# A recurrent attention block with an MLP: new order of the weight stream and of the V bounces at the start, residual sums in four pieces at the MLP

## Chip, cores, metric

One core of one Trainium2 chip. The metric is the time of one execution in device microseconds (us). A time is the median of several executions; every execution quoted here, of every kernel, was in the fast state. Times within a profile count from the start of its span.

## The reference, cut to what matters

```python
# S = 2048 rows of 512, 32 heads of 128, M = 8 memory rows, segments of 32 rows: 64 segments
for s in range(n_seg):
    h = concat([mem, x[:, s*32:(s+1)*32]])           # 40 rows
    q, k, v = h @ Wq, h @ Wk, h @ Wv                   # 512 -> 32 heads x 128
    p = softmax(where(mask, q @ k.T * scale, -1e9))
    o = (p @ v) @ Wo                                   # 4096 -> 512
    mem = o[:, :M]                                     # the next segment needs it
    outs.append(o[:, M:])
h  = x + concat(outs)                                  # raw x here; the x in the loop is layer-normed
h2 = h + gelu(layernorm(layernorm(h)) @ w1 + b1) @ w2 + b2     # MLP, 1792 wide
```

The 64 segments are a chain, since each needs the memory rows of the one before. The kernel takes x in 16 blocks of 128 rows (four segments each); q, k and v of a block's x rows are computed a block ahead ("block passes"), those of the memory rows within the segment.

## The kernel before

Three things matter. First, **the start**: SP (SyncE's queue) loads the weights as sixteen pieces of 1 MB, WK, WV, WQ and WO, in that order and as fast as it can issue. PE (TensorE) works through START.

```python
START = (("B", "K", 0, (4, 6)), "K0", "K1", ("B", "K", 1, (4, 6)), ("B", "V", 0, (6, 7)), "V",
         ("B", "V", 1, (6, 7)), ("B", "Q", 0, (5, 6)), "Q0", "Q1", "Z",
         "SC0", "SC1", ("B", "Q", 1, (5, 4)), "PV0", "PV1", "SA", "WO")
...
load_x(0, load)
load(...m0...); load(...b1n...)
load_w(WK, wk_d, "WK")          # four pieces of 1024 KB
load_x(1, load)
load_w(WV, wv_d, "WV")
load_w(WQ, wq_d, "WQ")
for g in range(4): load(... WO[:, g*8:(g+1)*8, :] ..., 1024, ...)
for tb in (2, 3, 4): load_x(tb, load)
```

Second, **the bounce of V**. PV needs the V rows of a block in another layout than the matmul leaves them in. They are evicted to VSB, sent to HBM (v_last, four DMAs of 64 KB, the first leg) and read back as VBD (four more, the second leg; the leg's part number sg serves only segment 4*block + sg):

```python
def v_B_spread(bk):
    for i in range(4):
        S.dma(... vd[bk, :, i] <- VSB[:, i] ..., 64, reads=[("VSB", r) for r in range(2)],
              eng="act" if bk < 2 else "sp")
    for sg in range(4):
        S.dma(... VBD[:, bk % 2, sg] <- vd[bk] part sg ..., 64, reads=[("vd", bk, i) for i in range(4)],
              eng="act" if bk < 2 else "sp")
```

Third, **the residual sums at the MLP**: h + b2 for a block of 512 rows is one GpSimd instruction of 128x2048 elements; the first stands ahead of the MLP in the program, the second at its step fc 3 (fc counts the MLP's 14 pieces of 128 columns), and both run in the MLP's first 11 us.

```python
def p2_res(k):
    S.op("pool", lambda e: e.tensor_tensor(hb[:, k % 2], hx_of(k), b2b, ALU.add), ...)
```

Every operation is registered with its reads, writes and an estimated duration, and the program's own list scheduler fixes each engine's order from them. A small change therefore may reorder several engines.

## Time and profile before

| | before |
|---|---|
| median (range), first set | 908.75 us (906.79 to 914.81), 3 runs |
| span of the profile | 909.0 us |
| PE busy | 827.0 us, 91% |
| end of segment 0 (transposition of its WO result starts) | 69.76 us |
| end of segment 1 | 82.83 us |
| end of segment 63 | 789.08 us |
| first W1 matmul, 17th W2 matmul | 793.35 us, 817.09 us |

The span is a start of 83 us, a chain of 62 segments (11.04 to 12.97 us each, 11.4 in the mean), and an MLP that is bound by PE. Only the ends have slack. The prediction shows the lines that say so. One more view is needed later: the issues of SP in the timeline of the start (start, length of the issues together, operation, count). The issuing itself takes long: WQ's four issues 11 us and WO's 19.

```profile
11.32 11.02 SPq L520 DMA_DIRECT2D WQ<-in_A_Wq_dram  x4
22.39 19.09 SPq L531 DMA_DIRECT2D WO<-in_A_Wo_dram  x4
```

### The profile page before, as it was taken

What the parts mean: (1) busy time and instruction counts of PE and PEld (TensorE: products, weight loads), DVE (VectorE), ACT (ScalarE), POOL (GpSimd) and SP (SyncE); (2) the same over time, 40 slices, a digit from 0 to 9 for tenths busy, and PEclk for the clock granted to TensorE, in tenths of its full rate; (3) what the DMA queues carried; (4) which work ended last, traced back from release to release, by engine and by line L of the source; (5) the groups of instructions that cost most, each with busy time, mean ns of one, the idle gap of its engine ahead of it and who ended that gap; (6) DMA issues with size and microseconds to landing.
All of it is one profiled execution on the core that took longest, in us unless ns stands there. A gap on an engine that the chain in (4) does not pass through costs nothing.

```text
span 909.0 us, 47688 instructions
## 1 busy us (share of the span) xinstructions
PE 827.0 (91%) x22285; PEld 436.4 (48%) x21261; DVE 659.3 (73%) x1801; ACT 522.2 (57%) x1520; POOL 222.6 (24%) x293
## 2 busy tenths in 40 slices
PE   1638899999999999999999999999999998889998
PEld 0214455555545555545555545555555554444443
DVE  2328788888888988897888898888797988661111
ACT  1224676656666767665757666767665666534442
POOL 3014222232222222222222222222222223141100
PEclk9858999999999999999999999999999999999999
DMA  8930001010101010101010101010101110610000
GB/s 334 388 112 3 4 4 27 10 33 15 27 16 28 16 27 16 27 16 27 16 27 15 27 15 27 10 28 9 27 10 27 33 27 9 209 39 24 24 24 23
DMA packets 35301, 40.42 MB, mean 44 GB/s; under 512 B 2452, under 2 KB 31004, under 8 KB 35100
## 3 DMA queue, kind: packets, MB, share of 16 engines
q1 hardware_dynamic: 32892, 36.33, 12.0%
q8 instruction: 170, 2.79, 1.3%
q10 hardware_dynamic: 2208, 1.05, 0.4%
q14 instruction: 31, 0.25, 0.1%
HBM read 28.98 MB, written 8.39 MB: 41 GB/s over the span
## 4 chain that ended last, share of the span: by engine, by line
PE 71%; ACT 15%; DVE 7%; DMA 3%; issue 2%; ACTq 1%; SPq 0%; POOL 0%; DVEq 0%
PE ps L583 27%; PE ps L826 15%; ACT VS L605 7%; PE ps L595 7%; PE ps L367 6%; PE quad L1076 6%; PE ps L1069 5%; ACT EC L727 4%; ACT OT L605 3%; DVE kqT L625 2%; DMA v_last<-VSB 2%; PE quad L798 2%; PE quad L745 2%; DMA xr<-in_A_x_dram 1%; DVE WV L933 1%
## 5 line engine op out<-in xcount | busy, mean ns | idle before, releaser
L640 POOL TENSOR_SCALAR QA<-kqT 128x384 bf16<-128x384 f32 x128 | 150.2, 1174 | 478.3 <-PE ps L583 324.4
L625 DVE STREAM_TRANSPOSE kqT<-ps 128x512 f32<-128x512 f32 x320 | 218.1, 710 | 28.6 <-PE ps L583 18.7
L826 PE MATMUL ps<-WO,OT 128*32 128x256 bf16 x4224 | 154.4, 277 | 14.3 <-ACT OT L605 5.1
L605 ACT CAST KALL<-kqT 128x512 bf16<-128x512 f32 x160 | 98.6, 618 | 82.2 <-DVE kqT L625 80.8
L583 PE MATMUL ps<-WK,hT 128*32 128x512 bf16 x2048 | 134.9, 384 | 3.6 <-DVE hT L832 3.3
L583 PE MATMUL ps<-WQ,hT 128*32 128x512 bf16 x2048 | 134.4, 383 | 0.0
L605 ACT CAST OT<-quad 128x128 bf16<-128x128 f32 (+1 forms) x176 | 80.2, 456 | 81.7 <-PE quad L749 46.6
L826 PEld LDWEIGHTS ps<-WO,OT 128*32 128x32 bf16 x4224 | 96.7, 96 | 45.9 <-ACT OT L605 33.5
L595 PE MATMUL ps<-WV,hT 128*32 128x512 bf16 x1024 | 100.7, 382 | 0.9
L367 PE MATMUL ps<-WV,hT 128*32 128x512 bf16 x1024 | 99.9, 379 | 0.0
L583 PEld LDWEIGHTS ps<-WQ,hT 128*32 128x32 bf16 x2048 | 54.6, 98 | 58.5 <-issue 2.5
L727 ACT ACTIVATE EC<-ps,nmc 128x64 f32<-128x64 f32 x256 | 78.1, 314 | 0.6 <-DVE nmc L723 0.6
L605 ACT CAST VS<-ps 128x512 bf16<-128x512 f32 x127 | 68.2, 589 | 11.7 <-PE ps L583 2.6
L1072 ACT ACTIVATE WQ<-ps,b1t 128x512 bf16<-128x512 f32 x56 | 38.5, 688 | 62.1 <-PE ps L1069 61.6
L583 PEld LDWEIGHTS ps<-WK,hT 128*32 128x32 bf16 x2048 | 49.3, 97 | 49.6 <-DVE hT L832 4.6
L699 ACT COPY ps<-maskCF 128x128 f32<-128x128 f32 x122 | 32.8, 269 | 62.2 <-DVE kqT L625 33.7
L1120 DVE TENSOR_TENSOR WV<-quad,WV 128x512 bf16<-128x512 f32 x16 | 11.1, 692 | 74.3 <-PE quad L1076 74.3
L715 PEld LDWEIGHTS ps<-KALL,ZC 128*32 128x32 bf16 x2048 | 34.7, 97 | 57.5 <-ACT ZC L606 48.0
L838 DVE STREAM_TRANSPOSE TT<-ps 128x256 f32<-128x256 f32 x66 | 29.3, 444 | 37.8 <-PE ps L826 37.8
L1076 PE MATMUL quad<-WK,WQ 128*128 128x512 bf16 x224 | 56.1, 388 | 0.5 <-DVE xr L872 0.5
L595 PEld LDWEIGHTS ps<-WV,hT 128*32 128x32 bf16 x1024 | 27.3, 96 | 60.3 <-DVE kqT L625 29.9
L727 ACT ACTIVATION_READ_ACCUMULATOR EC<-ps,nmc 128x1 f32 x256 | 52.4, 205 | 0.0
(107 smaller groups left out, 1218.3 us busy)
## 6 DMA issues: line engine op xcount, KB each, us to landing
WK<-in_A_Wk_dram SPq DMA_DIRECT2D x4, 1024.0 KB, 6.9
WV<-in_A_Wv_dram SPq DMA_DIRECT2D x4, 1024.0 KB, 19.0
WQ<-in_A_Wq_dram SPq DMA_DIRECT2D x4, 1024.0 KB, 19.0
WO<-in_A_Wo_dram SPq DMA_DIRECT2D x4, 1024.0 KB, 15.3
v_last<-VSB SPq DMA_DIRECT2D x56, 64.0 KB, 2.1
VBD<-v_last SPq DMA_DIRECT2D x56, 64.0 KB
WK<-in_B_w_dram SPq DMA_DIRECT2D x2, 1792.0 KB, 13.2
xr<-in_A_x_dram SPq DMA_DIRECT2D x16, 128.0 KB, 2.1
```

What stands on the lines that cost most here:

```text
L367: return e.add_instruction(mybir.InstMatmult(name="I-%d" % (4000000 + _kept[0]), engine=mybir.EngineType.PE, start_tensor_calc=start, stop ...
L583: ins = e.matmul(ps[bank][32 * j:32 * j + 32, :], lhs(cc), rhs(W, r, cc, j), start=(cc == 0), stop=(cc == DC - 1), tile_position=(0, 32 * j))
L595: ins = e.matmul(o, l, m, start=(cc == 0), stop=(cc == DC - 1), tile_position=(0, 32 * j))
L605: return {"act": (lambda e: e.copy(out, src), t_act(n, ps_)), "dve": (lambda e: e.tensor_copy(out, src), 0.16 + 1.042e-3 * n * fast)}
L625: S.op("dve", lambda e: e.transpose(kqT[:, i, :], ps[bank][:, :]), reads=[("ps", bank)], writes=[("kqT", i)], dur=t_dve(512) + 0.02)
L640: S.op("pool", lambda e: e.tensor_scalar(QA[:, h0:h0 + 16, 0:NA], src[:, :, 0:NA], scale, None, ALU.mult), reads=[("kqT", i)], writes=[("Q ...
L715: ins = e.matmul(ps[bank][32 * j:32 * j + 32, 64 * sl:64 * sl + 64], ZC[:, par, h, :], rhs, start=False, stop=(i == 3), tile_position=(0, ...
L727: ins = e.activation(EC[:, r, sl, :], ps[bank][:, 64 * sl:64 * sl + 64], ACTF.Exp, bias=nmc[:, r, sl:sl + 1], accum_out=smc[:, r, sl:sl + 1])
L826: ins = e.matmul(ps[bank][32 * j:32 * j + 32, 0:256], lhs(slot(h)), wo_cols(h, b), start=(k == 0), stop=(k == 15), tile_position=(0, 32 * ...
L1069: ins = e.matmul(ps[bank][:, 0:SBT], W1[:, cc, fc * P:(fc + 1) * P], hnT_of(k)[:, cc, :], start=(cc == 0), stop=(cc == DC - 1))
L1072: S.op("act", lambda e: e.activation(gT[:, fc, :], ps[bank][:, 0:SBT], ACTF.Gelu_apprx_tanh, bias=b1t[:, fc:fc + 1], scale=1.0), reads=[(" ...
L1076: S.op("pe", lambda e: e.matmul(quad[:, t, :], gT[:, fc, t * P:(t + 1) * P], W2[:, fc, :], start=(fc == 0), stop=(fc == FC - 1)), reads=[" ...
```

## The change

Intent: let V go first, so that its bounce is hidden behind the other weights; take the bounce off ACT, which stood in its queue for it; keep no more than three weight pieces under way, so that a bounce is not queued behind ten of them; and take the long GpSimd sums out of the place where DVE normalizes for the MLP. The core of the diff; "..." and comments stand for what is cut:

```diff
-START = (("B", "K", 0, (4, 6)), "K0", "K1", ("B", "K", 1, (4, 6)), ("B", "V", 0, (6, 7)), "V", ("B", "V", 1, (6, 7)), ("B", "Q", 0, (5, 6)), "Q0", "Q1", "Z",
-         "SC0", "SC1", ("B", "Q", 1, (5, 4)), "PV0", "PV1", "SA", "WO")
+START = (("B", "V", 0, (6, 7)), "V", ("B", "K", 0, (4, 6)), "K0", "K1", ("B", "K", 1, (4, 6)), ("B", "Q", 0, (5, 6)), "Q0", "Q1", "Z",
+         "SC0", "SC1", ("B", "Q", 1, (5, 4)), "PV0", "PV1", "SA", ("B", "V", 1, (6, 7)), "WO")
...
         def load(fn, kb, writes):
-            first[0] = S.dma(fn, kb, writes=writes, behind=first[0])
+            after = [big[-3]] if kb > 1000 and len(big) > 2 else []     # at most three pieces under way
+            o = S.dma(fn, kb, writes=writes, after=after)
+            chain.append(o)
+            if kb > 1000:
+                big.append(o)
...
+        load_w(WV, wv_d, "WV")
+        load_x(1, load)
         load_w(WK, wk_d, "WK")
-        load_x(1, load)
-        load_w(WV, wv_d, "WV")
         load_w(WQ, wq_d, "WQ")
...
         # both legs of the bounce: eng="act" if bk < 2 else "sp" is gone, all on SP; kept in spread["out"/"in", bk]
...
+                for what, n in ((("in", 0), 11), (("out", 0), 8)):
+                    i = chain.index(big[n - 1]) + 1          # out: behind the 8th piece (WK's last)
+                    chain[i:i] = spread[what]                # in: behind the 11th (WQ's third)
+                chain += spread["out", 1] + spread["in", 1]
+                for a_, b_ in zip(chain, chain[1:]):
+                    b_.prev = a_
...
         # a WO unit reads only its own two of the four WO pieces
...
         def p2_res(k):
-            S.op("pool", ... hb[:, k % 2] <- hx_of(k) + b2b, after=used["WV"] + S.users([("PTA", (NS - 1) % 2)]), dur=t_pool(2048))
+            for t in range(TBS):
+                S.op("pool", ... hb[:, k % 2, t, :] <- hx_of(k)[:, t, :] + b2bc, after=used["WV"] + S.users([("rs2", NTB - 1)]), dur=1.1)
...
-        p2_res(0)                       # was ahead of the MLP; now every block's sums stand at fc 8,
...                                     # the next block's norms at fc 8 (3 before), its transposes at fc 12 (9 before)
```

More of the change, by code (lines that the diff above doesn't have):

```diff
@@ L510, in load_x @@
             load(lambda e: e.dma_start(xr[:, tb % XR, :], x_d[:, tb, :]), 128, writes=[("xr", tb % XR)])
-        first = [None]
+        big = []
         def load(fn, kb, writes):
-            first[0] = S.dma(fn, kb, writes=writes, behind=first[0])
+            after = [big[-3]] if kb > 1000 and len(big) > 2 else []
[3 more added lines that the diff above has]
+                big.append(o)
+        chain, spread = [], {}
         def load_w(W, wd, key):
@@ L672, in v_B_spread @@
                 o = vd[bk, :, i]
-                S.dma(lambda e, i=i, o=o: e.dma_start(o, VSB[:, i].rearrange("p r e -> p (r e)")), 64, reads=[("VSB", r) for r in range(2)], writes=[("vd", bk, i)],
-                      eng="act" if bk < 2 else "sp")
+                w = S.dma(lambda e, i=i, o=o: e.dma_start(o, VSB[:, i].rearrange("p r e -> p (r e)")), 64, reads=[("VSB", r) for r in range(2)], writes=[("vd", bk, i)])
+                spread.setdefault(("out", bk), []).append(w)
             for sg in range(4):
                 v = vd[bk].rearrange("(j s) i t n -> s j (i t) n", s=4)[sg]
-                S.dma(lambda e, sg=sg, v=v: e.dma_start(VBD[:, bk % 2, sg].rearrange("p r e -> p (r e)"), v), 64, reads=[("vd", bk, i) for i in range(4)], writes=[("VBD", bk % 2, sg)],
-                      eng="act" if bk < 2 else "sp")
+                w = S.dma(lambda e, sg=sg, v=v: e.dma_start(VBD[:, bk % 2, sg].rearrange("p r e -> p (r e)"), v), 64, reads=[("vd", bk, i) for i in range(4)], writes=[("VBD", bk % 2, sg)])
+                spread.setdefault(("in", bk), []).append(w)
         def build_masks(bank_c, bank_a):
@@ L828, in f @@
                     return ins
-                S.op("pe", f, reads=[("WO", g) for g in range(4)] + reads(q // 4), writes=[("ps", bank)], dur=0.22, mode=MC, ni=16)
+                S.op("pe", f, reads=[("WO", 2 * (q // 4) + g) for g in range(2)] + reads(q // 4), writes=[("ps", bank)], dur=0.22, mode=MC, ni=16)
         def halves_add(tt, q2, out, cols):
@@ L908, in build_kernel @@
         hnT0 = bass.AP(kq45.tensor, kq45.offset, [list(kq45.ap[0]), [SBT, DC], [1, SBT]])
-        b2b = bass.AP(b2bc[:].tensor, b2bc[:].offset, [list(b2bc[:].ap[0]), [0, TBS], [1, D]])
         used = {"WQ": [], "WK": [], "WV": []}
@@ L936, in p2_res @@
         def p2_res(k):
-            S.op("pool", lambda e: e.tensor_tensor(hb[:, k % 2], hx_of(k), b2b, ALU.add), reads=[("hx", bf_of(k)), "b2bc"], writes=[("hb", k % 2)],
-                 after=used["WV"] + S.users([("PTA", (NS - 1) % 2)]), dur=t_pool(2048))
+            for t in range(TBS):
+                S.op("pool", lambda e, t=t: e.tensor_tensor(hb[:, k % 2, t, :], hx_of(k)[:, t, :], b2bc[:], ALU.add), reads=[("hx", bf_of(k)), "b2bc"],
+                     writes=[("hb", k % 2, t)], after=used["WV"] + S.users([("rs2", NTB - 1)]), dur=1.1)
         def p2_T(k, half, bank):
@@ L1108, in build_kernel @@
                         p2_load(k + 1)
-                    if fc == 3 and k + 1 < NSB:
+                    if fc == 8:
+                        p2_res(k)
+                    if fc == 8 and k + 1 < NSB:
                         p2_norm(k + 1)
-                        p2_res(k + 1)
-                    if fc == 9 and k + 1 < NSB:
+                    if fc == 12 and k + 1 < NSB:
                         p2_T(k + 1, 0, 7)
@@ L1120, in build_kernel @@
                 S.op("dve", lambda e, t=t, bf=bf: e.tensor_tensor(ob[:, bf, t, :], quad[:, t, :], hb[:, bf, t, :], ALU.add),
-                     reads=[("ps", t), ("hb", bf)], writes=[("ob", bf, t)], after=used["WV"], dur=t_dve(512))
+                     reads=[("ps", t), ("hb", bf, t)], writes=[("ob", bf, t)], after=used["WV"], dur=t_dve(512))
                 S.dma(lambda e, tb=tb, t=t, bf=bf: e.dma_start(out_d[:, tb, :], ob[:, bf, t, :]), 128, reads=[("ob", bf, t)], writes=[("out", tb)])
```

## The prediction

> **What bounds the kernel now.** First the page's part 2, 40 slices of 22.7 us, to find where TensorE is not the limit:
>
> ```profile
> PE   1638899999999999999999999999999998889998
> ...
> PEclk9858999999999999999999999999999999999999
> DMA  8930001010101010101010101010101110610000
> ```
>
> TensorE is 90% busy or more from slice 6 on. It is not in slices 1 to 5, where the DMA engines are full (8, 9) and then idle while PE is still at 3 and its clock at 5, and again in slices 34 to 36 (750 to 818 us), where the MLP begins. The change touches just these two places. In between lie 63 recurrent segments: the chain that ended last shows the same two V evictions in each, 11.05 to 11.2 us apart, and nothing in the diff shortens that.
>
> For the start I read busy time by stretches of 2 us (columns: stretch, length, busy time of PE, PEld, DVE, ACT, POOL, clock, DMA share, GB/s):
>
> ```profile
> 34.00:36.00 2.00, 1.04 (x16) 0.33 (x16) 0.72 (x1) 0.00 (x0) 0.00 (x0) 1.00 1.03 391
> ...
> 48.00:50.00 2.00, 0.00 (x0) 0.00 (x0) 0.00 (x0) 0.02 (x1) 0.00 (x0) 0.50 1.11 344
> ...
> 54.00:56.00 2.00, 0.00 (x0) 0.00 (x0) 0.00 (x0) 0.00 (x0) 0.00 (x0) 0.50 0.20 65
> ...
> 68.00:70.00 2.00, 1.72 (x35) 1.08 (x24) 1.52 (x6) 0.00 (x0) 0.79 (x2) 0.50 0.00 0
> ```
>
> Until 36 us weights come at about 400 GB/s; the stream ends at about 51 us. Yet no engine works between 48 and 58 us, and the clock stays halved to 75 us. So the stream sets the floor, and something else costs time beyond it. What that is stands in the chain of waits (start, length, what):
>
> ```profile
> 32.70 6.60 DMA v_last<-VSB
> ...
> 39.39 0.59 ACT VSB L605
> ...
> 46.72 9.08 DMA v_last<-VSB
> ...
> 58.22 0.64 ACT QTB L606
> ...
> 60.10 3.44 PE ps L583 x32
> ...
> 66.15 3.59 PE ps L826 x48
> ```
>
> The V rows of a block go to HBM and back (VSB to v_last to VBD). For blocks 0 and 1 ACT issues both legs. It stands in its own queue until the first leg has landed, and the evictions behind it wait too: VSB of block 1 to 39.39, and QTB of block 0, whose input was ready by 46, to 58.22. ZC, the scores and all of segment 0 hang on QTB. The waits view agrees: ACT QTB waited 14.4 us in two waits, the longest 10.2, named "issue".
>
> For the other end, the timeline of the MLP's beginning:
>
> ```profile
> 795.98 4.06 POOL L937 TENSOR_TENSOR WV<-xr,b2bc 128x2048 f32<-128x2048 bf16 x1 [10.90 <-DVE PTA L789]
> 796.73 8.19 DVE L933 TENSOR_SCALAR WV<-WQ,agg,rst 128x512 bf16<-128x512 bf16 x4
> ...
> 805.48 1.38 DVE L933 TENSOR_SCALAR WV<-WQ,agg,rst 128x512 bf16<-128x512 bf16 x4
> ...
> 810.16 0.40 PE L863 MATMUL quad<-ident,opT 128*128 128x128 bf16 x4 [2.87 <-DVE opT L854]
> ...
> 811.07 5.31 PE L1076 MATMUL quad<-WK,WQ 128*128 128x512 bf16 x16 [0.51 <-DVE xr L872]
> ```
>
> The same four normalizations take 8.19 us beside two residual sums on POOL (to 804.1) and 1.38 us without. The DVE work that PE needs (opT, TTB) is late by that much: PE stands still 2.87 and 0.51 us, and then runs 16 matmuls in 5.31 us at a clock that the stretches give as 0.52 and 0.63.
>
> **What the Trainium skill says.** (1) "DMA: Bandwidth & Descriptors", section "Anatomy of one DMA": DMA engines do not wait on semaphores; a wait happens on the issuing sequencer before dispatch. The trace agrees: the whole ACT queue stood 9.08 us. (2) Same page, "Queues, rings and completion order": each engine consumes a ring's descriptors in ring order. So behind SP's weights a bounce will not be quick either; a cap of 3 MB bounds the queue ahead of it. Here 64 KB legs took a median of 9.8 us to land in the start and 2.1 later. (3) "SBUF — State Buffer", section "SBUF: two separate sides": DVE in a two-port mode and GpSimd share a port pair by an exclusive lock, and the loser blocks for the whole instruction. The trace agrees: L933 lasts 407 ns in the median and 4160 at most, a POOL sum 4060. (4) "TensorE: Matmul & The Clock Gate", Part 1: half clock after an idle window of some 3.4 us, full clock after one of sustained work. Here 32 matmuls take 1.90 us in the start when warm and 3.44 at 60 us.
>
> **The change, part by part.**
>
> (a) V first, ACT freed, bounces in SP's queue. The bytes stay, so I count landings. The GB/s of the 2 us stretches, summed, give 4.0 MB by 14 us, 8.9 by 26, 13.0 by 36 and 17.2 by 48; a landing is seen about 2 us later (x1, the last of 4.46 MB, landed at 17.17, the sum reaches that at 15.1). In the new order: WV complete near 16.5 us (4.3 MB), WK near 27 (8.9 MB with x1 and the first leg), WQ near 39 (13.4 MB with both legs), WO near 51 (17.6 MB).
>
> V of block 0 ends about 0.9 us after WV (8 cold matmuls); with 0.6 for the eviction VSB stands by 18.2. The first leg's slot comes after WK's last piece is issued, which waits for WK's first to land (about 19.5); four issues of 0.6 us are done at 22 and land near 27.5. The second leg (four of 0.53) is issued near 30 and lands before WQ does, long before PV needs it. Neither slot leaves fewer than about two pieces (2 MB, 5 us) under way, so I expect no hole in the stream.
>
> PE from WQ on, in its order: Q of block 0, last 8 matmuls, at 39.0 to 39.9; Q0 and Q1, 32 matmuls, cold 3.5 us (warm 1.9), to 42.5; transpose 0.72 and ZC 0.30, scores to 44.7; softmax (0.28, 1.0, 0.17, 0.3, 0.3 and hops) to 47, beside Q of block 1; PV, SA to 49.5; V of block 1, 32 matmuls now warm 1.9, to 51.5; WO, 64 matmuls at 1.93 warm or 3.6 cold, from 51.5 since its last piece lands near 51. End of segment 0: 53.4 to 55.5, I take 54.5. Before it was 69.74. **Gain 15.2 us.**
>
> (b) Segment 1 warm. Its WO transposition came 13.07 us after that of segment 0 (69.76 to 82.83), where later segments take 11.05: **2.0 us**, if PE is busy enough from 45 us on.
>
> (c) WO units read only the two WO pieces they use: this matters in segment 0 alone and is in (a).
>
> (d) Residual sums in four pieces and after the last rs2. They leave 796 to 804. The first L933 group falls from 8.19 to about 1.6. Then PE's own work sets the pace: from 793.35 it has 8 fc of W1 at 0.86, three WO passes at 1.93, PV 0.3 and two transposes at 0.4, in sum 13.8 us, to about 807.2; the last transposes need TTB and opT, ready by 806.6; then L872 (0.42) and hops: W2 begins at 808.1 instead of 811.07, **3.0 us**. An idle time of 0.5 us does not halve the clock: 16 matmuls at 0.216 are 3.46 us for 5.31, **1.85 us**. The sums themselves (four of about 1.05 us for one of 4.06) fall where DVE has little to do, and the L1120 adds that need them come near 825. Blocks 1 to 3 of the MLP run back to back in 25.25 us each; their sums, norms and transposes (now at fc 12) have more than 4 us of slack: 0.
>
> Sum: 15.2 + 2.0 + 3.0 + 1.85 = 22.0. I take off 1.3, because the program's own list scheduler orders all engines anew from estimated times, and such an order seldom meets the best case: about 20.7 of 908.75, so **888.0 us**.
>
> **Rivals.** First, **the stream as the new bound, later than I count**: a cap of three means that each issue waits for a receipt, and a bounce leg that isn't ready holds SP and all weights behind it. The ready times above speak against it, but the margins are about 1 us at the second leg. Holes of 1.5 us at several pieces would put WO at 57 to 60 us: gain of the start 9 to 11, time 894 to 897. Second, **the wait moves into the compute chain**: PE gets Q as the last but one, with half a clock, and Q, scores, softmax, V of block 1 and WO come one after the other; if PE stays cold through segment 1, (a) loses 2 and (b) goes: 891 to 892. Third, **POOL takes DVE's place at the end**: the eight small sums meet the later norms and the rs2 chain; then (d) brings 1 to 2 instead of 4.85: 891. For more than I count: if PE stays warm through Q, segment 0 ends at 52 and the time is 884 to 885. No rival reaches 908.
>
> **Range and chances.** All of the gain is in two windows that are plainly idle, so slower needs a fault of the new order in the 63 segments, 0.2 us each for 12 us. Low end 880: everything warm, plus some luck in the segments. High end 897: holes in the stream, or the tail gives nothing. 2% lies at 890.6, just inside my middle: faster 0.68, within 2% 0.31, slower 0.01.
>
> **What would show it.** Right: no ACT wait on v_last in the first 60 us; VSB of block 0 evicted by 20 us; WQ's last matmuls starting at 37 to 41 us; segment 0's last WO matmul at 52 to 57; a full clock from about 50 us; the DMA row without a slice below 300 GB/s before 45 us; all L933 under 1.5 us each; W2 of the first MLP block starting 14 to 16 us after its first W1, and 16 of its matmuls in 3.5 us. Wrong: SP waiting on VSB or on v_last with fewer than two weight pieces under way; PE below full clock at 60 us; the mean distance of segments changed by over 0.1 us; L1120 or the norms waiting for POOL.

## The result, and the profile after

| | before | after |
|---|---|---|
| median (range), same rounds | 909.71 us (906.79 to 914.81), 4 runs | 900.94 us (899.39 to 901.91), 4 runs |
| ratio of the fast runs | | 0.9896, 95% interval 0.9847 to 0.9945 |
| span of the profile | 909.0 | 898.3 |

All ratios here are the mean time of one kernel's fast runs over that of the other's fast runs of the same rounds, so not quite the ratio of the medians. The gain is 1%, about half of what was predicted, and the time is outside the predicted range.

Where it came from, by profile (us):

| stretch | before | after | gain | predicted gain |
|---|---|---|---|---|
| start, to the end of segment 1 | 82.83 | 72.71 | 10.1 | 17.2 |
| segments 2 to 63 | 706.25 | 710.64 | -4.4 | 0 |
| end of segment 63 to first W1 matmul | 4.27 | 4.55 | -0.3 | 0 |
| first W1 to 17th W2 matmul | 23.74 | 18.51 | 5.2 | 4.85 |
| from there to the end | 91.87 | 91.87 | 0 | 0 |

The tail did what was predicted, and the start fell short by 7 us. (The 4.4 us lost in the segments are chance, as the repeats below show.) The page's rows of after, in 40 slices: in the slice from 45 to 67 us (the third digit) PE is at 7 where it was at 3, but the one before it has gone from 6 to 5, and the clock there from 8 to 7.

```profile
PE   2578999999999999999999999999999998889998
...
PEclk9789999999999999999999999999999999999999
DMA  8860000000001010101010101010101110421000
```

The chain that ended last, in its first 61 us, tells why (start, length, what the chain hung on):

```profile
8.31 8.55 DMA xr<-in_A_x_dram
...
19.43 0.58 PE quad L559 x4
20.02 3.56 PE ps L589 x32
...
24.21 0.63 SPq L679
...
26.16 3.79 DMA v_last<-VSB
...
31.59 3.06 SPq L683
...
35.24 9.84 DMA WQ<-in_A_Wq_dram
...
55.53 3.34 PE ps L589 x32
58.87 1.77 PE ps L832 x64
```

Read it from the top. After WV's first issues the chain turns to the second x block: its load, issued at 8.31 behind all of WV, lands at 16.86, it is normalized, and PE transposes it at 19.43. Only then does V of block 0 (L589) begin, at 20.02, though its weights had been there since about 17 (in e1 below PE takes the last of them at 17.04). SP, which stands at the first leg's slot, gets to issue it at 24.21 (L679), and after three pieces of WQ waits for the leg to land (29.95), issues the second leg, one part of which takes 3.06 us to issue (L683), and only at 35.24 comes to WQ's last piece. That lands at 45.08. At the end V of block 1 (55.53) takes 3.34 us, at half clock, ahead of WO, whose last piece landed at 57.21. The windows of 2 us show the two holes that this makes in the weight stream (the last two columns are the DMA share and GB/s):

```profile
24.00:26.00 2.00, 1.82 (x28) 0.21 (x8) 0.14 (x1) 0.33 (x2) 0.00 (x0) 1.00 0.71 268
26.00:28.00 2.00, 1.50 (x28) 0.76 (x32) 0.96 (x2) 0.44 (x1) 0.00 (x0) 1.00 0.48 121
28.00:30.00 2.00, 2.00 (x44) 1.00 (x40) 1.71 (x3) 1.24 (x2) 0.00 (x0) 1.00 0.82 190
...
36.00:38.00 2.00, 1.04 (x8) 0.14 (x8) 0.72 (x1) 0.04 (x1) 0.00 (x0) 0.50 0.62 244
38.00:40.00 2.00, 1.04 (x8) 0.17 (x8) 0.00 (x0) 0.59 (x1) 0.00 (x0) 0.50 0.36 97
```

At the other end, the timeline of PE (start, length, matmuls) answers to the line with 5.31 us of before:

```profile
787.16 0.29 PE L832 MATMUL ps<-WO,OTB 128*32 128x256 bf16 x2 [3.00 <-issue]
...
802.10 3.63 PE L1090 MATMUL quad<-WK,WQ 128*128 128x512 bf16 x16 [0.52 <-DVE xr L878]
```

The idle time of 2.87 us ahead of W2 is gone, 16 W2 matmuls take 3.63 us for 5.31, and each of the norms (L938) lasts 371 to 414 ns, where the longest of before was 4160. The first line is another matter: PE stands 3.00 us in the middle of a group of WO matmuls that waits for nothing. It does so in the kernel before too (2.94 us), and the prediction overlooked it.

### The profile page after: what moved, and what is told of

Same layout as the page of the kernel before. It is cut to its first block, busy times and chain, and to the rows that moved or that the text cites. A ratio compares the mean times of both kernels' runs of the same rounds, so it can differ in the third digit from the quotient of the medians.

```text
span 898.3 us, 47685 instructions
## 1 busy us (share of the span) xinstructions
PE 822.1 (92%) x22271; PEld 433.7 (48%) x21261; DVE 652.2 (73%) x1801; ACT 521.9 (58%) x1520; POOL 223.7 (25%) x305
## 3 DMA queue, kind: packets, MB, share of 16 engines
q8 instruction: 170, 2.79, 1.3%
HBM read 28.98 MB, written 8.39 MB: 42 GB/s over the span
## 4 chain that ended last, share of the span: by engine, by line
PE 72%; ACT 15%; DVE 6%; DMA 3%; issue 3%; SPq 1%; POOL 0%; DVEq 0%
PE ps L589 27%; PE ps L832 15%; ACT VS L611 7%; PE ps L601 7%; PE ps L367 6%; PE ps L1083 5%; PE quad L1090 5%; ACT EC L733 4%; ACT OT L611 3%; DVE kqT L631 2%; PE quad L804 2%; PE quad L751 2%; DMA WQ<-in_A_Wq_dram 1%; DMA xr<-in_A_x_dram 1%; PE ps L721 1%
## 5 line engine op out<-in xcount | busy, mean ns | idle before, releaser
L589 PE MATMUL ps<-WK,hT 128*32 128x512 bf16 x2048 | 133.3, 380 | 3.9 <-DVE hT L838 3.6
L589 PE MATMUL ps<-WQ,hT 128*32 128x512 bf16 x2048 | 134.0, 382 | 0.0
L589 PEld LDWEIGHTS ps<-WQ,hT 128*32 128x32 bf16 x2048 | 54.7, 98 | 57.7 <-DVE kqT L631 2.4
L589 PEld LDWEIGHTS ps<-WK,hT 128*32 128x32 bf16 x2048 | 49.0, 96 | 48.4 <-DVE hT L838 3.3
L1086 ACT ACTIVATE WQ<-ps,b1t 128x512 bf16<-128x512 f32 x56 | 38.5, 688 | 57.2 <-PE ps L1083 56.8
L1090 PE MATMUL quad<-WK,WQ 128*128 128x512 bf16 x217 | 53.7, 379 | 0.9 <-DVE xr L878 0.5
```

Source lines behind the costliest of these rows:

```text
L589: ins = e.matmul(ps[bank][32 * j:32 * j + 32, :], lhs(cc), rhs(W, r, cc, j), start=(cc == 0), stop=(cc == DC - 1), tile_position=(0, 32 * j))
L1086: S.op("act", lambda e: e.activation(gT[:, fc, :], ps[bank][:, 0:SBT], ACTF.Gelu_apprx_tanh, bias=b1t[:, fc:fc + 1], scale=1.0), reads=[(" ...
L1090: S.op("pe", lambda e: e.matmul(quad[:, t, :], gT[:, fc, t * P:(t + 1) * P], W2[:, fc, :], start=(fc == 0), stop=(fc == FC - 1)), reads=[" ...
```

## The experiments

Two theories were tested first. **Theory**: V of block 0 is late because x1's transposes stand ahead of it in PE's order and x1 is loaded behind WV; the bounce leg that isn't ready holds SP and with it all weights. **Rivals**: the cap of three pieces makes the stream slow; SP is the wrong queue for the bounces; or the gain was lost in the 63 segments.

Abbreviations: S0 and S1 are the ends of segments 0 and 1 in the profile (before 69.76 and 82.83; after 60.66 and 72.71). Kernels of a set ran on the same chip beside the kernel before, whose median was 909.49 in set A, 909.34 in B, 910.07 in C and 912.01 in D.

### e0_repeat (A) and e13_repeat2 (C): the changed kernel again

No edit.

> The changed kernel once more, as the yardstick of this set and to see whether the 63 segments are 4.4 us longer each time (72.71 to 783.36, against 82.83 to 789.08 before, between the first and the last segment's WO transposition). The order of all instructions of DVE, ACT and POOL between them is the same in both kernels. If the extra is chance of one execution, the distance of segments in this profile should differ from 710.65 by some us; if the new start causes it, it should be within 1 us of it. Time about 900.

> The changed kernel once more, in the same rounds as the two others, for an interval: 896 to 901 us, 9 to 12 us under the kernel before, segment 0 ends at 59.5 to 60.7.

| | median us (range) | ratio | S0 | S1 | segments 2 to 63 | W1 to 17th W2 |
|---|---|---|---|---|---|---|
| first run of after | 900.94 (899.39 to 901.91) | 0.9896 | 60.66 | 72.71 | 710.64 | 18.51 |
| e0 | 896.68 (895.17 to 906.01) | 0.9894 | 59.51 | 70.72 | 706.48 | 19.37 |
| e13 | 899.8 (897.35 to 901.19) | 0.9888 | 63.75 | 75.50 | 705.97 | 20.19 |

The ratio is the same three times. The segments at 706 us equal those of before (706.25), so the 4.4 us lost in the first profile were chance, and the order of instructions on DVE and ACT there is the same. S0 spreads from 59.5 to 63.75 with one and the same program (59.5 to 60.7 was expected of e13): e13 met the half clock in nearly all of the Q and V matmuls of its start (three groups of 32 took 3.63, 3.40 and 3.22 us, where 1.9 is the time at full clock). Single profiles are good to some 4 us here, no better.

### e1_x1_first (A): x1 ahead of the weights

```diff
         load_x(0, load)
+        load_x(1, load)
         ...
         load_w(WV, wv_d, "WV")
-        load_x(1, load)
```

> One line moved: x of block 1 is loaded right after x of block 0, ahead of WV. My theory: PE's queue holds the transposes of block 1 ahead of V of block 0, x1 landed only at 16.9 us behind WV, so V began at 19.95 and VSB stood at 24.2 instead of 18.2; SP, waiting for VSB, issued no weights meanwhile. If so: V's first matmul before 12 us, VSB evicted by 18.5, no 2 us stretch under 300 GB/s between 24 and 32, WQ's last matmuls start at 39 to 41 instead of 45.1, segment 0's WO transposition at 54 to 57 instead of 60.66, time 4 to 6 us under the changed kernel. Rival (the cap of three starves the stream by itself): the holes stay though VSB is early, and the time falls by under 2 us.

896.31 us (894.24 to 897.41), ratio 0.9853 (0.9827 to 0.9878). The first half of the theory holds: V began at 11.38, the first leg was issued at 19.97, as soon as SP was through with WK, and no window from 24 to 32 us is under 390 GB/s. The timelines of PE (first line) and SP:

```profile
11.38 1.90 PE L589 MATMUL ps<-WV,hB 128*32 128x512 bf16 x16
...
22.61 5.82 SPq L526 DMA_DIRECT2D WQ<-in_A_Wq_dram  x3
28.98 3.10 SPq L683 DMA_DIRECT2D VBD<-v_last  x4
32.12 3.34 SPq L526 DMA_DIRECT2D WQ<-in_A_Wq_dram  x1
```

But WQ's last matmuls began at 41.54 and S0 was 58.96, over the expected 39 to 41 and 54 to 57, because the second hole stayed, at 32 to 38 us. The second leg's slot lies between WQ's third and fourth piece. SP waits there for the first leg to land (to 28.98), then takes 3.10 us for four parts of 64 KB and 3.34 us for the issue of one weight piece, which takes 0.37 us elsewhere. When that is through, at 35.46, one earlier piece is left under way, and the window of 34 to 36 us has 110 GB/s. The time did not show what the stream won: the median is 0.4 us under e0's, the ratio 0.4% lower, and the intervals overlap; 4 to 6 us were expected.

### e5_x1_no_cap (B): e1 without the cap

```diff
-            after = [big[-3]] if kb > 1000 and len(big) > 2 else []
+            after = []
```

> x1 first as in the run before, and the cap of three pieces in flight taken away; the slots stay. Theory: the holes come from what SP waits for and issues at the two slots, not from the cap, so segment 0's WO transposition comes within 1.5 us of 58.96 and the time within 2 us of that run (896.3). Rival: the cap's receipts starve the stream: without it WQ's last matmuls start 3 us earlier or more (41.5 with the cap) and the time falls by 3 us.

898.67 us (896.0 to 899.81), ratio 0.9877 (0.9852 to 0.9901), S0 59.41. The same hole, the same slow issues (WQ's last 3.31 us). The cap neither causes the hole nor is it worth anything that can be seen: the two ratios differ by 0.0024, about 2 us, less than their intervals (within 2 us of e1 was expected).

### e6_x1_slot12 (B): e1 with the second leg behind WQ's last piece

```diff
-                for what, n in ((("in", 0), 11), (("out", 0), 8)):
+                for what, n in ((("in", 0), 12), (("out", 0), 8)):
```

> x1 first, and the second bounce leg one place later: after the last WQ piece instead of before it. Theory: in the run with x1 first the one hole left (110 GB/s at 34 to 36 us) comes from this leg: SP waits for the first leg to 28.9, four issues take to 32.1, and WQ's last piece is then 3.3 us in issuing. With it ahead of the leg, WQ's last matmuls start at 38 to 40 instead of 41.54 and segment 0's WO transposition comes at 56 to 57.5 instead of 58.96; time 1.5 to 3 us lower. Rival: only the place of the hole moves (to WO's pieces, which segment 0 waits for as well) and the transposition stays within 0.7 us of 58.96.

894.95 us (891.84 to 897.83), ratio 0.9839 (0.9804 to 0.9874), S0 55.78, S1 67.46. WQ's last piece was issued at 30.51, its matmuls began at 38.20. The hole moved behind it: 137 and 154 GB/s from 36 to 40 us, between WQ and WO, and WO landed at 53.48. S1 is 3.4 us earlier than in e1, the time only 1.4 us less (1.5 to 3 were expected): in this profile segments 3 and 4 took 11.83 and 13.07 us, at a clock that had halved once more. e5 and e15 show the same at the same place, e11 and e12 don't.

### e7_act_bounces (B): V first, the bounces of blocks 0 and 1 on ACT as before

```diff
-  ... VBD and v_last DMAs on SP, at places 8 and 11 of the weights
+  ... eng="act" if bk < 2 else "sp", no places in the weights' chain
```

> The changed kernel, but the bounces of blocks 0 and 1 issued by ACT again, as before, so SP's queue holds weights alone; V still first, V of block 1 still after SA. It tells the order of V from the move of the bounces. If the move to SP's slots is what cost (holes), WQ's last matmuls start at 36.5 to 39 instead of 45.1 and segment 0's WO transposition comes at 55 to 58 instead of 60.66, though ACT stands for some us around 30 with nothing urgent behind it. If freeing ACT is what gained, ACT's stand delays K, ZC or segment 1, and segment 1's WO transposition comes later than 72.7.

898.42 us (896.87 to 900.68), ratio 0.988 (0.9854 to 0.9905), S0 57.33, S1 70.89. The weights now flow without a hole to 36 us, and ACT pays instead (timeline of ACT):

```profile
24.48 2.60 ACTq L679 DMA_DIRECT2D v_last<-VSB  x4
...
34.98 3.01 ACTq L684 DMA_DIRECT2D VBD<-v_last  x4
38.03 3.22 ACT L611 CAST KALL<-kqT 128x512 bf16<-128x512 f32 x6 [10.32 <-issue]
```

ACT stands 10.3 us ahead of the K evictions, and again by block 1's legs; segment 1 takes 13.56 us. In the end it is as fast as the change. So the start's gain does not need the move of the bounces: taking them from ACT to SP, at the places that the change gives them, trades one wait for another, and the time is the same within the intervals. The gain goes with what e7 keeps of the change: V first, V of block 1 behind SA, the cap, and WO units that read two pieces. V first is the likely cause, but no run takes these apart (of the cap alone e5 shows no effect).

### e9_fill (B): e6 with Q and V of block 1 as fill work of segments 1 and 2

```diff
-         "SC0", "SC1", ("B", "Q", 1, (5, 4)), "PV0", "PV1", "SA", ("B", "V", 1, (6, 7)), "WO")
+         "SC0", "SC1", "PV0", "PV1", "SA", "WO")
+                if s == 1: kq_B(1, 1, r, BANK["F%d" % r])
+                if s == 2: v_B(1, r, BANK["F%d" % r])
```

> A version that should beat both: x1 first, second leg after WQ, and Q and V of block 1 taken out of the start and put into the fill places of segments 1 and 2, which are empty there. Theory: segment 0's chain (PV waited for Q of block 1, WO for V of block 1, 3.2 to 3.4 us each at half clock) then ends with WO's last piece: WO transposition at 53 to 55.5, segment 1's at 64 to 67.5, time 5 to 8 us under the changed kernel. Rival: PE idles more, stays at half clock into segment 1, and segments 1 and 2 become longer than 11.05 by the fill: under 3 us.

896.65 us (894.87 to 899.24), ratio 0.9868 (0.9842 to 0.9894), S0 55.64, S1 68.62. Nothing was gained, as its rival said (5 to 8 us under the changed kernel were expected): with less work in segment 0, PE waits 4.1 us for WO's last piece and stays at the clock 0.50 from 44 to 60 us, and segment 1 takes 12.98 us. Here, with WO landing at 53.56, the stream is the bound.

### e11_one_part (C): e1, and only the part of the second leg that segment 0 reads stands in the weights

```diff
-                for what, n in ((("in", 0), 11), (("out", 0), 8)):
+                spread["in0"] = spread["in", 0][:1]
+                for what, n in (("in0", 12), (("out", 0), 8)):
...
-                chain += spread["out", 1] + spread["in", 1]
+                chain += spread["in", 0][1:] + spread["out", 1] + spread["in", 1]
```

> x1 first; of the second bounce leg of block 0 only the part that segment 0 reads (one of four issues) stands behind WQ's last piece, the other three behind the x loads at the end of the stream. Theory (what is left of the hole at 32 to 40 us is SP standing in four short issues, of 0.5 to 2.8 us each, with only one or two weight pieces under way): WQ's last matmuls near 38 us as with slot 12, no 2 us stretch under 250 GB/s between 30 and 42 us, WO's last piece landed near 50 to 51 instead of 53.5, end of segment 0 near 53 to 54 instead of 55.8 (as the prediction had it: 54.5), time 1 to 2 us under the slot-12 version's 894.95, so 893 to 894. Rival (the DMA engines are the limit, and the hole is a pause that is made up later because bytes per us after it are higher): WO lands at 53 again and segment 0 ends at 55 to 56.

889.74 us (888.38 to 894.41), ratio 0.979 (0.9759 to 0.9821), beside 0.9888 (0.9858 to 0.9918) for the changed kernel in the same set: the fastest version found, 10 us under the change (whether it is over 2% faster than the kernel before its interval just leaves open). The stream has no hole any more:

```profile
36.00:38.00 2.00, 0.60 (x8) 0.10 (x8) 0.00 (x0) 0.00 (x0) 0.00 (x0) 0.77 1.08 356
38.00:40.00 2.00, 1.33 (x16) 0.53 (x20) 0.14 (x1) 0.00 (x0) 0.00 (x0) 0.50 1.11 329
```

The last WQ matmuls began at 38.67 and WO landed at 51.19, just where the prediction's stream has them (39 and 51). S0 came at 55.87, later than the expected 53 to 54, and here the clock decides. The timeline of PE in e11, and below it in e12, which has the same program up to the MLP:

```profile
44.70 3.18 PE L589 MATMUL ps<-WQ,hB 128*32 128x512 bf16 x32
...
50.48 3.44 PE L589 MATMUL ps<-WV,hB 128*32 128x512 bf16 x32
```

```profile
44.78 1.90 PE L589 MATMUL ps<-WQ,hB 128*32 128x512 bf16 x32
...
49.28 1.92 PE L589 MATMUL ps<-WV,hB 128*32 128x512 bf16 x32
```

Block 1's Q and V at half clock or at full clock make S0 55.87 or 52.99. Nothing in the program differs up to there, so this is when the clock happened to rise. (e11's profile is of the slowest of its six executions, 894.41 us; the S0 of the faster ones is not known.)

### e2_mlp_only (A) and e3_start_only (A): each half of the change alone

e2 is the kernel before with the MLP part of the diff, e3 the changed kernel with that part undone.

> The kernel before with only the MLP part of the change (residual sums in four pieces after the last rs2, norms at fc 8, transposes at fc 12). Theory: the shared port is freed, the stretch from the first W1 matmul to the end of the first 16 W2 matmuls falls from 23.0 to about 17.8 us, and the time falls by 4.5 to 5.5 us against the kernel before. Rival: the MLP part gives nothing by itself since the instruction stall of 3 us ahead of it or the DVE chain absorbs it: under 2 us.

> The changed kernel with the MLP of the kernel before. Theory: the start gives 10.1 us up to segment 1's WO transposition, so the time is 5 us above the changed kernel and, if the segments really take 4.4 us more, only 5 to 6 us under the kernel before; if the longer segments are chance, 9 to 10 under it.

e2: 906.28 us (903.57 to 910.87), ratio 0.9972 (0.9954 to 0.9989), some 2.5 us; expected were 4.5 to 5.5. e3: 900.44 us (896.03 to 902.28), ratio 0.9894 (0.9859 to 0.9928), with S1 at 72.44; it was expected 5 us above the changed kernel, and its ratio is that of e0, its median 3.8 us above. The start makes up nearly all of the change. In e2's profile the stretch from W1 to the 17th W2 matmul is 20.83 us, not 18.5: the stop of 3 us after segment 63, seen above, this time halved the clock, and 64 WO matmuls took 3.60 us for 1.93.

```profile
790.38 0.39 PE L826 MATMUL ps<-WO,OTB 128*32 128x256 bf16 x1 [3.25 <-issue]
...
792.85 3.60 PE L826 MATMUL ps<-WO,OT 128*32 128x256 bf16 x64
```

So the predicted 4.85 us are there when the clock holds (after: 18.51 us), and some 3 of them when it does not: the stretch took 18.5 to 20.8 us in the ten profiles with this MLP order and whole loads. The MLP of before varies too: 23.74 us in its own profile, 21.64 in e3's.

### e12_one_part_pieces (C): e11, with W1 and W2 in eight pieces, two under way

What is the stop of 3 us? It falls into the load of 3.67 MB of W1 and W2. In after, the DMA view of 784 to 785.5 us, inside the stop, has one packet of the instruction queue (16 KB by the profile's page, where 170 of them make 2.79 MB) among 503 packets of data, on engines that are full (packets, MB, share):

```profile
q1 hardware_dynamic: 503, 0.52, 106.1%
q8 instruction: 1, 0.02, 4.8%
```

```diff
-        S.dma(... W1 <- w1_d, 1792, after=used["WK"])
-        S.dma(... W2 <- w2_d, 1792, after=used["WK"])
+        # four pieces of 448 KB each; a piece waits for the last but one to have landed
```

> The kernel before this one, and W1 and W2 of the MLP in eight pieces of 448 KB, two under way, instead of two loads of 1792 KB. Theory (the stall of some 3 us of PE after segment 63, named issue, comes because PE's instructions are fetched behind 3.7 MB of weights in the DMA engines): with less ahead of it the stall falls to 1 to 1.5 us, the clock never halves there, first W1 to 17th W2 matmul takes 18 to 19 us, and the time is 1.5 to 2.5 us less. Rival (the stall belongs to the place in the program): still 3 us, same time, or W1 arrives late and it is longer.

893.39 us (887.68 to 895.49), ratio 0.9809 (0.9775 to 0.9844). The stop fell from 3.23 us (e11, first line) to 0.59 (e12, second fence):

```profile
779.67 0.28 PE L832 MATMUL ps<-WO,OTB 128*32 128x256 bf16 x2 [3.23 <-issue]
```

```profile
775.60 0.29 PE L832 MATMUL ps<-WO,OTB 128*32 128x256 bf16 x2 [0.59 <-issue]
```

So it goes with that load and not with the place in the program. In each of the twelve profiles with whole loads exactly one such packet starts in the stop, 0.2 to 1.0 us after its beginning; in e12 and e15 none does. That fits the theory, but that the packet holds PE's instructions, and that PE waited for it, is argued and not shown. The time was not won (from W1 to the 17th W2 it took 24.00 us, 18 to 19 were expected): the load of h for MLP block 1 now stands in SP's queue behind eight waiting pieces, the norms wait 7.27 us for it, the last opT is late by 3.48 us, the clock halves, and 16 W2 matmuls take 5.31 us as in the kernel before.

### e15_hx_first (D): e12 with that load of h between W1's and W2's pieces

```diff
+        hx1 = p2_load(1, behind=last_w[-1])       # behind W1's pieces, ahead of W2's
```

> The kernel with the pieces of W1 and W2, and the h rows of MLP block 1 loaded between W1's and W2's pieces instead of behind both. Theory (the pieces took the 3 us stall down to 0.6, but the load of the h rows, now behind all eight pieces in SP's queue, came 7.3 us late for the norms, which made the last opT late, PE idle for 3.5 us and its clock half for 16 matmuls): no PE idle above 1 us between segment 63 and the first W2 matmul, clock full there, segment 63 to 17th W2 matmul 21 to 22.5 us instead of 26.1 (with whole loads 24.9), time 887 to 890. Rival (DVE now stands for the h rows ahead of TTB, or the stall of 3 us comes again elsewhere): 24 to 26 us again, time 890 to 893.

896.32 us (893.53 to 898.58), ratio 0.9825 (0.9796 to 0.9853): the rival came true. The stop is 0.27 us, but the scheduler has put the norms ahead of the TTB transposition on DVE, and DVE stands for h (timeline):

```profile
780.98 1.38 DVE L938 TENSOR_SCALAR WV<-WQ,agg,rst 128x512 bf16<-128x512 bf16 x4 [2.83 <-DMA WQ<-h_mid]
...
782.86 3.60 PE L832 MATMUL ps<-WO,OT 128*32 128x256 bf16 x64 [2.81 <-DVE TTB L857]
```

A gap of 2.81 us and the half clock in its wake. From W1 to the 17th W2 it took 24.08 us. Pieces of weights as such are sound, but these two orders give back what they win. An order that keeps it was not found.

## Why the prediction was wrong, point by point

**The bound, right.** The two ends were where the time could be won, nothing changed in the segments (706 us in before, e0, e13, and in e2 and e3) and nothing in the last 92 us. One thing is open: the eight other orders of the start (e1, e5, e6, e7, e9, e11, e12, e15) took 707.2 to 712.0 us in segments 2 to 63, although in those compared (e1, e6, e11) DVE and ACT have the same order there. Half clock in segments 3 and 4 is part of it in three; no run says whether the rest is chance. So what a variant wins at S1 is not all in its time.

**Part (a), wrong, and by the step "V of block 0 ends about 0.9 us after WV (8 cold matmuls); with 0.6 for the eviction VSB stands by 18.2".** I counted V's weights and not what stands ahead of V in PE's order. The transposes of x block 1 do, and they need x1, which the change loads behind WV. V began at 19.95 and not with WV's first pieces, all 32 matmuls came after x1, and the first leg was issued at 24.21 instead of about 19.5. e1 shows the cause: with x1 first, V begins at 11.38 and the leg is issued at 19.97. Of the 6.1 us by which WQ's last matmuls came late (45.13 for 39), this step made about 3.6 (41.54 in e1) and the next one the rest (38.67 in e11).

**The step after it, "Neither slot leaves fewer than about two pieces (2 MB, 5 us) under way, so I expect no hole", wrong too, and on its own.** In e1, with V in time, the hole at the second slot is still there. SP stands at the slot until the first leg has landed, as predicted (28.98 us for "near 30"); what was mis-sized is the issuing. The four issues were taken at 0.53 us each, and they and the next weight issue took 3.10 and 3.34 us. When they were through, one earlier piece was left under way, not two. e6 moves that cost behind WQ and e11 takes three of the four parts out; then WQ and WO come at 38.67 and 51.19.

| step | predicted | after | e11, e12 |
|---|---|---|---|
| first leg issued | 19.5 | 24.21 | 20.19, 20.13 |
| last WQ matmuls begin | 39 | 45.13 | 38.67, 38.83 |
| WO landed | 51 | 57.2 | 51.19, 51.16 |
| end of segment 0 | 54.5 | 60.66 | 55.87, 52.99 |
| segment 1 | 11.05 | 12.05 | 11.63, 11.91 |

The last column shows that the rest of the sum of (a) was sound: given the stream that it assumed, segment 0 ends at 53 to 56 us, by the clock. That version runs in 889.74 us, where the prediction had 888.0 for the change; that they are so close is in part luck, since its profile has S1 at 67.50 for 65.6, and 20.36 us to the 17th W2 matmul for 18.9.

**The rival that came true** was named first, "the stream as the new bound ... a bounce leg that isn't ready holds SP and all weights behind it". I put it aside on ready times with margins of "about 1 us", and the first leg's was wrong by 4.7 us. Its figures for the start were right in the first profile: WO at 57 to 60 us (57.2), a gain of 9 to 11 us (10.1; 12.1 and 7.3 in the repeats). Two of its reasons were not: the cap's receipts cost nothing that can be seen (e5), and at the second slot it is the issuing more than the leg's landing that costs. Its time, 894 to 897, holds one of the three medians (896.68); it kept all of (d). **The second rival**, PE cold in segment 0, came in too: V of block 1, predicted warm at 1.9 us, took 3.5 in after and 3.2 in e13 (1.9 in e0), so that in after WO's matmuls began 1.5 us behind the landing of its last piece. Of the third, GpSimd in DVE's way at the end, the runs show no sign (norms under 0.42 us).

**Part (b), not shown.** Segment 1 took 12.05 us instead of 13.06, a gain of 1.0 for 2.0, and 11.21 in e0, 11.75 in e13. But the 13.06 was one execution's clock and not a cost of the program: e2 has the start of before and S0 at 69.41, and there segment 1 took 11.05 (PE at full clock from 70 us on, at half clock to 74 us in before). The prediction read a single profile as a rule; with e2 as the base, all gains at S1 are 2.4 us less.

**Part (c)** was counted in (a). Nothing was measured for it alone.

**Part (d), right in the first profile** (5.2 us for 4.85, W2's 16 matmuls 3.63 us for 3.46, norms under 0.42 us), smaller in the mean: alone it is worth some 2.5 us in e2. No run separates the four pieces from their later place. The term missing was the stop of 3 us at the start of the MLP, which stands in every kernel with whole loads, and which in some profiles halves the clock and takes back about 2 us.

**The sum.** In the three profiles of the changed kernel, the start gained 10.1, 12.1 and 7.3 us (S1) for the predicted 17.2, and the stretch to the 17th W2 matmul 5.2, 4.4 and 3.6 for 4.85. So most of what is missing (9 to 13 us by the medians) is the start, by the two holes and the half clock, and up to 1.3 us is the tail.

What stays open: why single issues of 64 KB parts and the weight issue behind them take 2.5 to 4 us. It goes with several such parts queued behind weight pieces, with and without the cap (e1, e5, e6), and is gone with one part (e11). But the kernel before has it with weights alone in SP's queue (WQ's fourth issue took 5.35 us, WO's second 9.93), so the parts need not be the cause; no run isolates it.

## What to carry to other kernels

To say when an operation starts, read what stands ahead of it in its engine's order, and the loads of those, not only its own operands: one small load placed behind 4 MB put V off by 8.6 us here (19.95 for 11.38). A transfer that needs another's result should not stand in the middle of a stream of weights; put it behind the last piece that is urgent, and only as much of it as the next consumer needs. And when a wait is moved from one queue to another, ask who stands behind it there: ACT's wait had become SP's, and the time was the same (e7).

## What the Trainium skill lacked or had wrong

- "DMA: Bandwidth & Descriptors", section "Issuing engines are not separate DMA queues", says that the time a sequencer takes to initiate a DMA "is usually small relative to the DMA itself". Here it is not: the same weight issue took 0.37 us with few transfers queued, and 3.3 to 4.1 us with four bounce parts just ahead of it (e1, e5, after, e13), and up to 9.93 us in the kernel before, behind weights alone; 64 KB parts took 0.5 to 3.55 us. No figure for a busy queue is on the page.
- "Runtime: NRT & Kernel Launch", section "Instruction fetch mechanics", calls the cost of crossing a block of instructions "mostly hidden". PE stopped for 2.9 to 3.6 us in every kernel that loads 3.67 MB at that point, with a 16 KB packet of the instruction queue among the data, and for 0.27 to 0.59 us with at most two pieces of 448 KB under way (e12, e15). If that packet is PE's, which no run shows, the cost is not hidden there.
- "TensorE: Matmul & The Clock Gate", Part 1, is right that the point where the clock rises varies, and that it costs under 1% of a typical span: the same program ended segment 0 at 52.99 and at 55.87 us (e12, e11), 2.9 us of 892. What it lacks is a measurement of stops somewhat shorter than its idle window: the clock halved after one of 3.25 us in e2, 2.87 in before and 2.81 in e15, and not after one of 3.00 in after.
- No page has the cost of a hop through HBM behind weights: a 64 KB part of the first leg landed 7.4 us after its issue in e11, against a median of 2.1 us over the whole of after.
